# Output weights loaded early into a buffer of their own, and two extra products in the first step

## The chip, the cores and the metric

The kernel runs on one core of a Trainium2 chip. The metric is the time of one execution in microseconds of device time; the median of the runs shown counts. The profile is one execution more, with the hardware profiler on.

## The reference

Two attentions over the same rows of `x` (2048 x 448, 16 heads of 28), mixed by a gate. Branch A looks at 8 earlier positions, two apart; branch B is full attention.

```python
g = _sigmoid((x * gate_w).sum(-1, keepdims=True))
a = _A_ref(x, A_wqkv, A_wo)     # 8 positions, dilation 2, softmax, then @ A_wo
b = _B_ref(x, B_wqkv, B_wo)     # softmax(q k^T / sqrt(28)) v over all 2048, then @ B_wo
return g * a + (1 - g) * b
```

## The kernel before

**Stages.** Up to about 252 us TensorE (PE) makes the projections q, k, v of both branches. Then comes a loop of 256 steps, `st` = 0 to 255. Sixteen steps make a unit `u`: one group of four heads (`g = u // 4`) with one block of 512 queries (`b = u % 4`); a step takes 128 keys. Every number is split into a high and a low part, so that a product of two needs three matmuls. While units run, the output projection starts at step 237 and ends after the loop.

**One step.** PE makes the scores (12 products with `QH`, `QL`, `KH`, `KL`, line 1041) into the PSUM tiles `T`, and ahead of time up to three products (line 144) whose maximum VectorE (DVE) takes into `MX` (line 148), for the maxima of a later unit. ScalarE (ACT) makes `exp` of the scores (`P`, line 1044, two instructions in a step). Then `do_av` multiplies the probabilities of the step before with `V` into the tile `av` (line 995, 8 products). Step 0 has no step before it and so no `do_av`. From step 235 on the products ahead of time are done; from step 237 on `op_some` adds five parts of the output projection to a step (line 835, three products a part).

**Finishing a unit** (`fin_*`, with the list `l` of steps after the unit's end). For unit 13 the steps count from 224. `fin_copy` copies `av` to `osb`; `fin_sum` and `fin_sum2` write the sums of the softmax to DRAM (`rs<-osb`) and read them back spread out (`fsum<-rs`); `fin_inv` takes the reciprocal on DVE (`finv<-fsum`, line 864) and multiplies it by the gate on GpSimd (POOL, line 865); `fin_spread` and `fin_spread2` write it to DRAM (`rs<-finv`) and read it back broadcast (`rbc<-rs`); `fin_on` multiplies on POOL (`on<-osb,rbc`, line 903); `fin_hi` (`onhi<-on` on ACT, line 907) and `fin_lo` (`onlo` on POOL) split it, and `fin_store` writes it to `on_hi`, `on_lo`.

**Branch A** runs beside this on POOL and DVE, by a planner's lists. When its lists are empty, `a_done(st)` frees its buffers and plans the output weights: `wo` has 7 blocks of 128 rows. `raw_wo(k)` loads a block into one of 7 buffers of 512 columns, `split_wo(k)` splits it on POOL (lines 778 and 779). Branch A's turned rows, stored by eight transfers `oa_scr<-oatT`, are read back by `op_load_a(b)` into buffers of the same 7 (`oar`) and split by `op_split`. The rows of branch B come back by `op_load_b` (`onhi<-on_hi`, `onlo<-on_lo`).

**What sets the order.** Each engine executes its instructions in the order in which the program was written. `at(pos, st, f)` hangs a function on a place in step `st`: "pre", "dve", "act" or "end". All transfers of the loop are issued by SyncE's queue (SP), in program order, and one that must wait holds those behind it.

Of the kernel before, what the change touches and what calls it, by code (L numbers as in the profile page):

```python
# [8 lines left out]
F32 = mybir.dt.float32  # L9
# [6 lines left out]
S, D, H, DH = 2048, 448, 16, 28  # L16
# [4 lines left out]
NU = NG * NB  # L21
# [4 lines left out]
def gated_mix_kernel(ctx: ExitStack, tc: tile.TileContext, xT, xn, gw, wA, wB, woAB, out):  # L26
    nc = tc.nc
# [45 lines left out]
    KH = [cp.tile([128, S], F32R, name=f"KH{i}") for i in range(2)]  # L73
# [45 lines left out]
    def load_q(u):  # L119
        Qs[u] = load_part(u, "QH", qk_hi), load_part(u, "QL", qk_lo)  # L120
        for i in range(2):
            dma_r(Qs[u][0][DH + i::32, :], nm[u][16 * i:16 * i + 16, :].rearrange("(h q) c -> h (q c)", h=4))
# [61 lines left out]
    def max_turn(t):  # L184
        r = sp.tile([128, 32], F32, name="nms")
        nc.vector.transpose(r, t)
        return r

    def max_store(u, r):
        for a in range(4):  # L190
            nc.sync.dma_start(nm[u].bitcast(F32)[:, 32 * a:32 * a + 32], r[32 * a:32 * a + 32, :])
# [14 lines left out]
    with tc.tile_pool(name="xp", bufs=1) as xp, tc.tile_pool(name="wp", bufs=2) as wp:  # L206
# [244 lines left out]
        for n, t in enumerate(tiles):  # L451
# [4 lines left out]
            for w in splits:  # L456
                i, k = (n - splits[w][0]) * splits[w][1], splits[w][1]
# [36 lines left out]
            if parts and parts[0][0] <= n:  # L494
                _, u, t = parts.pop(0)
# [25 lines left out]
    def at(pos, st, f):  # L521
        hooks.setdefault((st, pos), []).append(f)

    def run(pos, st):
        for f in hooks.pop((st, pos), ()):
            f()
# [10 lines left out]
    av = pool.tile([128, 512], F32, name="av")  # L537
# [35 lines left out]
    maskt = mp.tile([128, W, NJ, 2], F32, name="maskt")  # L573
    ep = ctx.enter_context(tc.tile_pool(name="ep", bufs=1))
    probs = [ep.tile([128, 2, 512], F32, name=f"P{i}") for i in range(4)]
    nc.gpsimd.memset(maskt, 0.0)
    for st, g, t, src in ((12, 2, KH[2], qk_hi), (30, 1, KL[1], qk_lo), (72, 2, KL[0], qk_lo),
                          (100, 3, KH[0], qk_hi), (136, 3, KL[1], qk_lo)):
# [118 lines left out]
    for c in range(8):  # L697
# [20 lines left out]
        n = 0  # L718
# [37 lines left out]


    wo = []
    wor = {}
    oP = {}  # L760

    def rawtile(name):
        return oP["0"].tile([128, 512], F32, tag="raw", name=name)

    def load_wo():
        actx.close()
        oP["0"] = ctx.enter_context(tc.tile_pool(name="rp", bufs=7))
        oP["1"] = ctx.enter_context(tc.tile_pool(name="wop", bufs=1))
        oP["2"] = ctx.enter_context(tc.tile_pool(name="wop2", bufs=2))
        wo.extend(oP["1"].tile([128, 7, D], F32R, name=f"wo{i}") for i in range(2))  # L770

    def raw_wo(k):
        wor[k] = rawtile("wor")
        nc.sync.dma_start(wor[k][:, :D], woAB[k])

    def split_wo(k):
        raw = wor.pop(k)[:, :D]
        nc.gpsimd.tensor_copy(wo[0][:, k, :], raw)
        nc.gpsimd.tensor_tensor(out=wo[1][:, k, :], in0=raw, in1=wo[0][:, k, :].bitcast(F32), op=ALU.subtract)  # L779

    def a_done(st):
        adone.append(st)
        load_wo()

        for i, k in enumerate((4, 5, 6, 0, 1, 2, 3)):
            at("end", st + i // 2, lambda k=k: raw_wo(k))
            at("act", st + 3 + i, lambda k=k: split_wo(k))
        at("end", st + 6, lambda: op_load_a(0))

    oaT, onT = {}, {}  # L790

    def op_load_a(b):
        cs = slice(512 * b, 512 * b + 512)
        for k in range(4):
            n = 128 if k < 3 else 64
            raws[b, k] = rawtile("oar")[0:n, :]
            nc.sync.dma_start(raws[b, k], oa_scr[128 * k:128 * k + n, cs])

    def op_split(b, k):
# [13 lines left out]
    raws = {}  # L813
# [35 lines left out]
    def fin_copy(u):  # L849
        t = mp.tile([128, 512], F32, name="osb")  # L850
        nc.scalar.activation(t, av, AF.Copy)  # L851
        fin["o"] = t


    def fin_sum(u):
        nc.sync.dma_start(rs_scr[0][u].rearrange("(h c) -> h c", h=4), fin["o"][DH::32, :])

    def fin_sum2(u):
        fin["s"] = sp.tile([128, 16], F32, name="fsum")
        nc.sync.dma_start(fin["s"], rs_scr[0][u].rearrange("(p i) -> p i", i=16))  # L860
# [7 lines left out]
    def fin_spread(u):  # L868
        nc.sync.dma_start(rs_scr[1][u].rearrange("(p i) -> p i", i=16), fin["rec"])

    def fin_spread2(u):
        fin["r"] = mp.tile([128, 512], F32, name="rbc")
        for h in range(4):
            nc.sync.dma_start(fin["r"][32 * h:32 * h + 32, :],
                                rs_scr[1][u][512 * h:512 * h + 512].rearrange("(o c) -> o c", o=1).to_broadcast(
                                    [32, 512]))
# [28 lines left out]
    def fin_hi(u):  # L905
        fin["hi"] = mtile("onhi").bitcast(F32R)
        nc.scalar.activation(fin["hi"], fin["on"], AF.Copy)
# [5 lines left out]
    def fin_store(u):  # L913
        g, b = divmod(u, NB)
        for dst, t in ((on_hi, fin["hi"]), (on_lo, fin["lo"])):
            for h in range(4):
                r = 112 * g + DH * h
                dma_r(dst[r:r + DH, 512 * b:512 * b + 512], t[32 * h:32 * h + DH])

    def pool_time(t, f, *x):  # L920
        late["pool"] += t
        f(*x)


    for u in range(NU - 1):
        f = NJ * (u + 1)
        l = {NU - 3: (1, 2, 5, 6, 9, 12, 13, 15), NU - 2: (1, 2, 5, 6, 8, 10, 10, 12)}.get(
            u, (1, 3, 6, 8, 12, 18, 19, 22) if u < NU - 5 else (1, 3, 6, 8, 12, 15, 16, 19))
        at("pre", f + 1, lambda u=u: fin_copy(u))
        at("end", f + l[0], lambda u=u: fin_sum(u))  # L930
        at("end", f + l[1], lambda u=u: fin_sum2(u))
        at("dve", f + l[2], lambda u=u: pool_time(0.18, fin_inv, u))
        at("end", f + l[2], lambda u=u: fin_spread(u))
        at("end", f + l[3], lambda u=u: fin_spread2(u))
        at("end", f + l[4], lambda u=u: pool_time(1.24, fin_on, u, fin["r"]))
        at("pre", f + l[5], lambda u=u: fin_hi(u))
        at("end", f + l[6], lambda u=u: pool_time(1.24, fin_lo, u, nc.gpsimd))
        at("end", f + l[7], lambda u=u: fin_store(u))
# [6 lines left out]
    def s1_close():  # L945
        accs.extend(sums(1 - turn[0]))
        side["f"] = accs[1]
        order.extend([*pbank[0], *sums(turn[0])])
# [43 lines left out]
    def do_av(pv):  # L992
        kt, tiles_, g = pv
        for h in (3, 2, 1, 0):
            nc.tensor.matmul(av[32 * h:32 * h + 32, :], V[:, kt, 4 * g + h, :], tiles_[h],  # L995
                             start=(kt == 0), stop=(kt == NJ - 1), skip_group_check=True)
# [81 lines left out]
    for u in range(NU):  # L1078
        g, b = divmod(u, NB)
        for kt in range(NJ):  # L1080
            st = NJ * u + kt
            if kt == (8 if u < 12 else 12) and u + 1 < NU:
                load_q(u + 1)
            run("pre", st)
            issue("sp", st, 0)
            if st >= A_START:
                issue("pool", st, 4.2)
            if not adone and not any(lists.values()):
                a_done(st)
            cur = {}  # L1090
            left = s1e - s1c[0]
            for a in scores(u, kt, cur):
                if a == 2:
                    run("mid", st)
            run("dve", st)
            if u and kt == 6:
                late["dve"] += 0.25
            if finished:
                v = finished.pop(0)
                t = max_parts(v)  # L1100
                late["dve"] += 0.3
                late["pool"] += 0.18
                turned = {}
                lag = 2 if v < NU - 1 else 1
                at("dve", st + lag, lambda t=t, w=turned: w.update(r=max_turn(t.bitcast(F32))))
                at("end", st + lag, lambda v=v, w=turned: max_store(v, w["r"]))
            issue("dve", st, DLIM)
            issue("act", st, 0)
            run("act", st)
            if prev is not None:  # L1110
                do_av(prev)
            prev = (kt, cur, g)
            if OPS and st >= OPS[0]:
                op_some(st, 5)
            run("end", st)
            step = 2.25 if left else 2.1
            late["dve"] = max(0.0, late["dve"] + 0.58 * min(3, left) - step)
            late["pool"] = max(0.0, late["pool"] - step)
            if st == OP0 + 31:
                op_load_b(2, 3)  # L1120
            if not OPS and s1c[0] == s1e:
                s1_close()
                for k in range(4):
                    at("act", st + 1 + k // 2, lambda k=k: op_split(0, k))
                OPS.append(st + 3)
# [55 lines left out]
```

## Time and profile before

| | |
|---|---|
| median of 3 runs | 913.0 us (911.75, 913.0, 913.59) |
| the profiled execution | 914.46 us, of which its span 912.6 us |
| PE busy | 901.7 us, 99% of the span |
| DVE, ACT, POOL busy | 740.2, 645.9, 626.3 us |
| mean granted TensorE clock | 0.996 |

A row of a timeline has the start from the beginning of the span, how long it lasted, engine, line, operation, tiles, shapes and count; in brackets stands the idle time of the engine just before it and what ended it. Equal instructions in a row are merged: the second number is then the time from the first's start to the last's end. Matmuls overlap, so a merged row is more telling than the duration of one.

### The profile page before, as it was taken

Reading aid. Unit: us, or ns where it says so; the run is one execution under the profiler, and the core shown is the slowest. Engines: PE = TensorE matmul, PEld = TensorE weight load, DVE = VectorE, ACT = ScalarE, POOL = GpSimd, SP = SyncE. Lnnn points to the kernel's source line nnn. Section 1 sums busy time; section 2 is a strip of 40 time slices with the busy share of each in tenths; the row PEclk is TensorE's granted clock in tenths of the full one; section 3 lists DMA queues with packets and bytes.
Section 4 is the critical chain, followed back from the end, with each engine's and each line's share of the span. In section 5 each row is a group of like instructions: output and inputs, shape, how many; then the busy total and the mean of one; then the engine's idle time right before and its main releaser. Section 6 shows DMA issues by size and latency. Waiting matters only on the chain.

```text
span 912.6 us, 20606 instructions
## 1 busy us (share of the span) xinstructions
PE 901.7 (99%) x8332; PEld 534.0 (59%) x8332; DVE 740.2 (81%) x997; ACT 645.9 (71%) x775; POOL 626.3 (69%) x494
## 2 busy tenths in 40 slices
PE   9999999999999999999999999999999999899998
PEld 7899999999944444444444444444444444366667
DVE  6488999999979999999999999999999988610112
ACT  6456434343378898898888888888989888744550
POOL 2489846564479699998999998899999293600100
PEclk9999999999999999999999999999999999999999
DMA  9887403554373341244144322532222222664323
GB/s 273 288 258 197 133 11 90 156 131 115 82 243 71 102 113 48 88 106 122 32 120 133 104 82 47 137 95 56 80 53 46 55 55 43 201 187 130 98 89 102
DMA packets 113919, 104.30 MB, mean 114 GB/s; under 512 B 74708, under 2 KB 82260, under 8 KB 113040
## 3 DMA queue, kind: packets, MB, share of 16 engines
q1 hardware_dynamic: 113680, 102.72, 40.2%
q8 instruction: 65, 1.06, 0.5%
q10 hardware_dynamic: 144, 0.26, 0.1%
q14 instruction: 30, 0.25, 0.1%
HBM read 61.99 MB, written 40.48 MB: 112 GB/s over the span
## 4 chain that ended last, share of the span: by engine, by line
PE 91%; DMA 3%; SPq 2%; ACT 1%; issue 1%; DVE 1%; POOL 0%; ACTq 0%; DVEq 0%
PE T L1041 28%; PE av L995 26%; PE r L298 15%; PE r L293 7%; PE T L835 7%; PE r L144 5%; PE T L144 4%; DMA onlo<-on_lo 1%; ACT P L1044 1%; SPq L101 1%; DMA rs<-finv 1%; DMA V<-in_xT 1%; SPq L680 1%; DMA oar<-oa_scr 0%; POOL wo L779 0%
## 5 line engine op out<-in xcount | busy, mean ns | idle before, releaser
L1044 ACT ACTIVATE P<-T 128x1024 f32<-128x1024 f32 x512 | 497.2, 1025 | 100.5 <-PE T L1041 99.1
L148 DVE TENSOR_REDUCE MX<-T 128x1 f32<-128x512 f32 x470 | 440.2, 952 | 24.2 <-PE T L144 13.1
L995 PE MATMUL av<-P,V 128*32 128x512 f32 x2048 | 273.6, 606 | 1.1 <-ACT osb L851 0.7
L1041 PEld LDWEIGHTS T<-QH,KH 30*128 30x128 f32 x1024 | 91.1, 182 | 225.2 <-ACT P L1044 201.7
L144 PE MATMUL T<-KH,QP 28*128 28x512 f32 x704 | 219.8, 455 | 0.5 <-DVE MX L162 0.3
L1041 PE MATMUL T<-QH,KH 30*128 30x512 f32 x1024 | 212.3, 490 | 2.4 <-ACT P L1044 1.7
L162 DVE TENSOR_REDUCE MX<-r 128x2 f32<-128x1024 f32 x160 | 192.5, 1220 | 24.7 <-PE r L144 23.1
L1041 PE MATMUL T<-QH,KL 28*128 28x512 f32 x1024 | 186.6, 397 | 0.0
L1041 PE MATMUL T<-QL,KH 28*128 28x512 f32 x1024 | 184.2, 394 | 0.0
L614 POOL TENSOR_TENSOR prod<-qt,kt 128x896 f32<-128x896 f32 x64 | 135.3, 2116 | 0.4
L362 ACT ACTIVATE raw<-r 128x896 f32<-128x896 f32 (+1 forms) x64 | 58.9, 920 | 97.9 <-PE r L298 96.6
L668 POOL TENSOR_TENSOR oat<-oat,prod 128x896 f32<-128x896 f32 x56 | 118.1, 2109 | 2.7
L144 PEld LDWEIGHTS T<-KH,QP 28*128 28x128 f32 x704 | 86.1, 182 | 28.0 <-ACT P L1044 20.6
L663 POOL TENSOR_TENSOR prod<-vt,L 128x896 f32<-128x896 f32 x56 | 95.3, 1702 | 0.5
L363 POOL TENSOR_TENSOR ast<-raw 128x448 f32<-128x448 f32 x48 | 55.4, 1154 | 58.2 <-ACT raw L362 46.0
L1041 PEld LDWEIGHTS T<-QL,KH 28*128 28x128 f32 x1024 | 93.8, 185 | 0.0
L1041 PEld LDWEIGHTS T<-QH,KL 28*128 28x128 f32 x1024 | 92.3, 183 | 1.0
L995 PEld LDWEIGHTS av<-P,V 128*32 128x32 f32 x2048 | 40.3, 108 | 79.3 <-issue 72.7
L144 PE MATMUL r<-KH,QP 64*128 64x512 f32 x320 | 85.6, 390 | 0.0
L298 PE MATMUL r<-wh,xh 64*128 64x448 f32 (+1 forms) x512 | 84.8, 362 | 0.0
L298 PE MATMUL r<-wh,xl 64*128 64x448 f32 (+1 forms) x384 | 69.7, 363 | 0.0
L298 PE MATMUL r<-wl,xh 64*128 64x448 f32 (+1 forms) x448 | 65.7, 367 | 0.0
(114 smaller groups left out, 1038.6 us busy)
## 6 DMA issues: line engine op xcount, KB each, us to landing
a_scr<-ast SPq DMA_DIRECT2D x24, 448.0 KB
qk_hi<-qkh SPq DMA_DIRECT2D x24, 256.0 KB
qk_lo<-qkh SPq DMA_DIRECT2D x24, 256.0 KB
rbc<-rs SPq DMA_DIRECT2D x60, 64.0 KB
QP<-qk_hi SPq DMA_DIRECT2D x64, 56.0 KB
KL<-qk_lo SPq DMA_DIRECT2D x16, 224.0 KB
QH<-qk_hi SPq DMA_DIRECT2D x64, 56.0 KB
QL<-qk_lo SPq DMA_DIRECT2D x64, 56.0 KB
```

Source lines behind the costliest of these rows:

```text
L144: nc.tensor.matmul(bank, qhis[u][h % 2][r, 128 * qs:128 * qs + 128], KH[u // NB % 3][r, 512 * kc:512 * kc + 512], start=True, stop=True)
L148: r = nc.vector.tensor_reduce(MX[:, n % NMX:n % NMX + k], bank, axis=X, op=ALU.max)
L162: nc.vector.tensor_reduce(m, PM[k], axis=X, op=ALU.max)
L293: nc.tensor.matmul(bank, ws[c][rows, k, t[4]:t[4] + 128], x, start=first, stop=last)
L298: nc.tensor.matmul(bank[:, 0:cols], x, ws[c][rows, k, 0:cols], start=first, stop=last)
L614: nc.gpsimd.tensor_tensor(out=p, in0=qt[c], in1=kvt["k", c % 2][:, HALO - DIL * w:HALO - DIL * w + NJ, :], op=ALU.mult)
L663: nc.gpsimd.tensor_tensor(out=dst, in0=kvt["v", c % 2][:, HALO - DIL * w:HALO - DIL * w + NJ, :].rearrange("p j (h d) -> p j h d", d=DH), ...
L668: nc.gpsimd.tensor_tensor(out=oat[c], in0=oat[c], in1=oat[c, w], op=ALU.add)
L835: writes(bank, nc.tensor.matmul(bank[:, :D], src, wo[c][:, k, :], start=(first and k == ks[0] and i == 0), stop=(last and k == ks[-1] and ...
L995: nc.tensor.matmul(av[32 * h:32 * h + 32, :], V[:, kt, 4 * g + h, :], tiles_[h], start=(kt == 0), stop=(kt == NJ - 1), skip_group_check=True)
L1041: nc.tensor.matmul(bank[a], (KH[g % 3], KH[g % 3], KL[g % 2])[t][r, ks], (qh, ql, qh)[t][r, :], start=(t == 0), stop=(t == 2))
L1044: e = nc.scalar.activation(p, RP[0] if a == "2" else mine, AF.Exp, scale=SCALE).ins
```

## The change

- `rawt`, 7 blocks of 448 columns, is a buffer of its own. Two transfers load all raw output weights into it, blocks 4 to 6 at step 200 and blocks 0 to 3 at step 202, instead of seven transfers in the steps after `a_done`.
- The splits of the weights stand two to a step, beginning one step after `a_done` instead of three.
- Branch A's turned rows are read back into the first 2048 columns of `rawt`, and for the first block one step earlier.
- For unit 13, `fin_inv` and `fin_spread` stand one step later (6 instead of 5) and `fin_spread2` as well (7 instead of 6).
- In step 0, where there is no `do_av`, two products of 128x512 are written to `av`; the next `do_av` overwrites them.

```diff
+    rawt = ep.tile([128, 7 * D], F32, name="rawt")
...
-        oP["0"] = ctx.enter_context(tc.tile_pool(name="rp", bufs=7))
...
-    def raw_wo(k):
-        wor[k] = rawtile("wor")
-        nc.sync.dma_start(wor[k][:, :D], woAB[k])
+    def raw_wo(k0, k1):
+        nc.sync.dma_start(rawt[:, D * k0:D * k1].rearrange("p (k c) -> p k c", c=D),
+                          woAB[k0:k1].rearrange("k p c -> p k c"))
...
+    at("end", 200, lambda: raw_wo(4, 7))
+    at("end", 202, lambda: raw_wo(0, 4))
...
         for i, k in enumerate((4, 5, 6, 0, 1, 2, 3)):
-            at("end", st + i // 2, lambda k=k: raw_wo(k))
-            at("act", st + 3 + i, lambda k=k: split_wo(k))
-        at("end", st + 6, lambda: op_load_a(0))
+            at("act", st + 1 + i // 2, lambda k=k: split_wo(k))
+        at("end", st + 5, lambda: op_load_a(0))
...
-            raws[b, k] = rawtile("oar")[0:n, :]
+            raws[b, k] = rawt[0:n, 512 * k:512 * k + 512]
...
-        l = {NU - 3: (1, 2, 5, 6, 9, 12, 13, 15), NU - 2: (1, 2, 5, 6, 8, 10, 10, 12)}.get(
+        l = {NU - 3: (1, 2, 6, 7, 9, 12, 13, 15), NU - 2: (1, 2, 5, 6, 8, 10, 10, 12)}.get(
...
             if prev is not None:
                 do_av(prev)
+            else:
+                for _ in range(2):
+                    nc.tensor.matmul(av, KH[0][:, 0:128], KH[0][:, 0:512], start=True, stop=True, skip_group_check=True)
```

Three places show how instructions move. On SP's queue, from branch A's last stores to the first loads for the output projection, before (`wor` are the raw weights, `oar` the turned rows):

```order
L680 DMA oa_scr<-oatT 448x1x32 x8
L856 DMA rs_13_81<-osb 4x512
L774 DMA wor<-in_wo 128x448 x2
L860 DMA fsum<-rs_13_81 128x16
L774 DMA wor<-in_wo 128x448 x2
L101 DMA on_hi<-onhi 28x512 x4
L101 DMA on_lo<-onlo 28x512 x4
L774 DMA wor<-in_wo 128x448 x3
L869 DMA rs_13_97<-finv 128x16
L874 DMA rbc<-rs_13_97 32x512 x4
L101 DMA onhi_10229<-on_hi 64x512
```

The same stretch of SP's queue with the change:

```order
L681 DMA oa_scr<-oatT 448x1x32 x8
L854 DMA rs_13_81<-osb 4x512
L858 DMA fsum<-rs_13_81 128x16
L101 DMA on_hi<-onhi 28x512 x4
L101 DMA on_lo<-onlo 28x512 x4
L867 DMA rs_13_97<-finv 128x16
L795 DMA rawt<-oa_scr 128x512 x3
L795 DMA rawt<-oa_scr 64x512
L872 DMA rbc<-rs_13_97 32x512 x4
L101 DMA onhi_10227<-on_hi 64x512
```

The weights are gone from here, and the four loads of turned rows, which stood behind the first loads of `onhi` and `onlo`, now stand between `rs<-finv` and `rbc<-rs`.

On POOL, the first splits of the weights and the reciprocal's product of unit 13, before:

```order
L668 TENSOR_TENSOR oat_3316<-oat_3316,prod_9873 128x32x28
L911 TENSOR_TENSOR onlo<-on,onhi 128x512
L778 CAST wo_10024<-wor 128x448
L779 TENSOR_TENSOR wo_10025<-wor,wo_10024 128x448
L865 TENSOR_TENSOR finv<-finv,og 128x16
```

With the change all seven pairs of splits come first; this is the last pair and what follows it:

```order
L774 CAST wo_10026<-rawt 128x448
L775 TENSOR_TENSOR wo_10027<-rawt,wo_10026 128x448
L863 TENSOR_TENSOR finv<-finv,og 128x16
L901 TENSOR_TENSOR on<-osb,rbc 128x512
L181 TENSOR_TENSOR nmt<-nmv,nmt 128x16
L909 TENSOR_TENSOR onlo<-on,onhi 128x512
```

So `finv` moved from behind one split to behind seven.

On PE, the end of step 0 and the beginning of step 1 with the change:

```order
L144 MATMUL T_3275<-KH_152,QP_158 128x512
L144 MATMUL T_3275<-KH_152,QP_157 128x512
L1039 MATMUL T_3271<-QH,KL_153 128x512 x2
L1112 MATMUL av<-KH_151 128x512 x2
L1039 MATMUL T_3279<-QH,KH_151 128x512 x2
L144 MATMUL T_3283<-KH_152,QP_158 128x512
```

The row of line 1112 is new; nothing else moved on PE.

## Rows read from the trace of the kernel before

**Rows 1.** Timeline of PE, steps 1 to 3 of the loop

```profile
255.43 0.50 PE L1041 MATMUL T<-QH,KH 30*128 30x512 f32 x2 [0.66 <-ACT P L1044]
...
257.08 1.94 PE L995 MATMUL av<-P,V 128*32 128x512 f32 x8
...
260.54 1.06 PE L995 MATMUL av<-P,V 128*32 128x512 f32 x8
...
262.83 1.07 PE L995 MATMUL av<-P,V 128*32 128x512 f32 x8
```

**Rows 2.** Windows of 1 us, PE: busy (count), granted clock, DMA share, GB/s

```profile
255.00:256.00 1.00, 0.57 (x8) 1.00 0.02 5
...
257.00:258.00 1.00, 1.00 (x10) 0.50 1.07 242
```

**Rows 3.** Timeline of PE, four full-width products of the projection

```profile
10.45 1.09 PE L293 MATMUL r<-xh,wh 128*128 128x512 f32 x4
```

**Rows 4.** Timeline of PE, beginnings of steps 231 and 232

```profile
777.41 0.50 PE L1041 MATMUL T<-QH,KH 30*128 30x512 f32 x2
...
779.26 0.50 PE L1041 MATMUL T<-QH,KH 30*128 30x512 f32 x2 [0.63 <-DVE MX L148]
...
781.15 0.50 PE L1041 MATMUL T<-QH,KH 30*128 30x512 f32 x2
```

**Rows 5.** Timeline of DVE, the reciprocal of unit 13

```profile
777.28 0.25 DVE L864 RECIPROCAL finv<-fsum 128x16 f32<-128x16 f32 x1 [1.83 <-DMA fsum<-rs]
```

**Rows 6.** Chain that ended last: start, us, what ran or was waited for

```profile
770.72 2.25 DMA oa_scr<-oatT
...
780.53 5.40 DMA rs<-finv
...
793.68 5.99 DMA onlo<-on_lo
...
823.89 3.23 PE T L835 x15
```

**Rows 7.** Timeline of POOL, splits of the weights and unit 13

```profile
775.86 0.56 POOL L778 CAST wo<-wor 128x448 fp32r<-128x448 f32 x1 [14.08 <-DMA wor<-in_wo]
...
777.61 0.22 POOL L865 TENSOR_TENSOR finv<-finv,og 128x16 f32<-128x16 f32 x1
777.77 0.56 POOL L778 CAST wo<-wor 128x448 fp32r<-128x448 f32 x1
...
779.48 0.55 POOL L778 CAST wo<-wor 128x448 fp32r<-128x448 f32 x1
...
789.58 1.27 POOL L903 TENSOR_TENSOR on<-osb,rbc 128x512 f32<-128x512 f32 x1 [1.40 <-DMA rbc<-rs]
```

**Rows 8.** Timeline of ACT, steps 235 and 236

```profile
788.90 1.94 ACT L1044 ACTIVATE P<-T 128x1024 f32<-128x1024 f32 x2 [0.15 <-PE T L1041]
790.89 0.63 ACT L907 ACTIVATE onhi<-on 128x512 fp32r<-128x512 f32 x1
791.69 1.94 ACT L1044 ACTIVATE P<-T 128x1024 f32<-128x1024 f32 x2 [0.16 <-PE T L1041]
```

**Rows 9.** Timeline of PE, first products of the output projection, then step 238

```profile
796.19 0.65 PE L835 MATMUL T<-wo,onhi 128*128 128x448 f32 x2 [0.54 <-issue]
...
802.62 0.52 PE L1041 MATMUL T<-QH,KH 30*128 30x512 f32 x4
```

**Rows 10.** Timeline of SP's queue, unit 11

```profile
705.73 0.34 SPq L869 DMA_DIRECT2D rs<-finv  x1
707.22 1.69 SPq L874 DMA_DIRECT2D rbc<-rs  x4
```

**Rows 11.** Timeline of POOL, unit 11

```profile
715.31 1.28 POOL L903 TENSOR_TENSOR on<-osb,rbc 128x512 f32<-128x512 f32 x1
```

**Rows 12.** Windows, all engines: PE PEld DVE ACT POOL busy, clock, DMA, GB/s

```profile
793.00:794.00 1.00, 0.62 (x6) 0.30 (x8) 0.86 (x1) 0.62 (x1) 0.99 (x1) 1.00 0.93 297
...
800.00:801.00 1.00, 1.00 (x5) 0.87 (x3) 0.00 (x0) 0.00 (x0) 0.00 (x0) 0.50 0.29 100
```

More of the change, by code (lines that the diff above doesn't have):

```diff
@@ L758, in gated_mix_kernel @@
     wo = []
-    wor = {}
     oP = {}
-    def rawtile(name):
-        return oP["0"].tile([128, 512], F32, tag="raw", name=name)
     def load_wo():
         actx.close()
-        oP["0"] = ctx.enter_context(tc.tile_pool(name="rp", bufs=7))
         oP["1"] = ctx.enter_context(tc.tile_pool(name="wop", bufs=1))
@@ L770, in load_wo @@
         wo.extend(oP["1"].tile([128, 7, D], F32R, name=f"wo{i}") for i in range(2))
-    def raw_wo(k):
-        wor[k] = rawtile("wor")
-        nc.sync.dma_start(wor[k][:, :D], woAB[k])
+    def raw_wo(k0, k1):
+        nc.sync.dma_start(rawt[:, D * k0:D * k1].rearrange("p (k c) -> p k c", c=D),
+                          woAB[k0:k1].rearrange("k p c -> p k c"))
     def split_wo(k):
-        raw = wor.pop(k)[:, :D]
+        raw = rawt[:, D * k:D * k + D]
         nc.gpsimd.tensor_copy(wo[0][:, k, :], raw)
         nc.gpsimd.tensor_tensor(out=wo[1][:, k, :], in0=raw, in1=wo[0][:, k, :].bitcast(F32), op=ALU.subtract)
+    at("end", 200, lambda: raw_wo(4, 7))
+    at("end", 202, lambda: raw_wo(0, 4))
     def a_done(st):
```

## Prediction

> **What bounds the kernel now.** I read the page first: PE is busy for 99% of the span, so time can only be won where PE waits or where its clock is low. Then I looked for such places in PE's timeline, asked the windows for the clock, and followed each wait back over DVE, ACT, POOL and SP. Three places bear on this change.
>
> *Step 1.* PE waits 0.66 us for ACT [rows 1]. Within 2 us the granted clock is 0.50, that is 1.2 instead of 2.4 GHz [rows 2], and the eight `av` products that take 1.06 us elsewhere take 1.94 [rows 1].
>
> *Step 231.* PE waits for DVE's maxima [rows 4]. DVE itself stood 1.83 us at the reciprocal of unit 13, for `fsum<-rs` [rows 5].
>
> *Steps 236 to 238.* ACT's `onhi` of unit 13 stands between the exponentials of two steps, and its input arrives with no slack: `on` ends at 790.85 (789.58 + 1.27) [rows 7], and ACT is free at 790.84 (788.90 + 1.94) [rows 8]. Then the first 15 products of the output projection take from 796.19 to 802.62 [rows 9], while 15 undisturbed ones take 3.23 us; the chain shows that a load of `onlo` was awaited until 799.67 (793.68 + 5.99) [rows 6], and the clock is at 0.50 again [rows 12].
>
> **The two products in step 0.** Four products of this width take 1.09 us [rows 3], so two take at most 0.55 us. They stand before step 1's scores, in the wait of 0.66 us, and need nothing that PE has not waited for. They cost nothing; without that cover, 0.55 us.
>
> What they can give is the clock. From `av` of step 0 to `av` of step 1 it is 3.46 us (260.54 - 257.08), and the next distance is 2.29 [rows 1]: the low clock costs 1.17 us. With 0.55 us of the wait filled, 0.1 us stays idle. In step 231 a wait of 0.63 us did not bring the clock down: the 1.89 us from its end to step 232 (779.26 to 781.15) [rows 4] leave no room for products at half speed. So the place in step 1 is just beyond what brings the clock down, and I take it that the clock stays up: **-1.2 us**. The bounds are -1.2 and 0.
>
> The Trainium skill (TensorE: Matmul & The Clock Gate, section on HAM oscillation in real kernels) ties the low clock to long waits for transfers between bursts of products. By that page a wait as short as this would not bring the clock down, the fillers would have nothing to prevent, and this term would be 0. The trace shows the low clock right behind the short wait, so the row decides for the sum.
>
> **The early load.** Two transfers are issued at steps 200 and 202, of 0.69 and 0.92 MB. The first falls into the wait of SP between `rs<-finv` and `rbc<-rs` of unit 11 (705.73 to 707.22) [rows 10]. At 297 GB/s, as in a busy stretch [rows 12], both together take 5.4 us. The data of `rbc` are used at 715.31 [rows 11], 6.4 us after its last issue (707.22 + 1.69). So it costs 0; without that cover some 2 us on POOL, which waits for DVE there anyway.
>
> **The stall at step 231.** The weights no longer stand in front of `fsum<-rs`, and DVE's reciprocal stands a step later. The wait of 1.83 us was counted from a point one step (2.29 us) earlier than where it now stands, so it is gone even if the transfer is no faster. Step 231 took 3.74 us (781.15 - 777.41) [rows 4] instead of 2.29. That is **-1.45 us** for PE and ACT in steps 231 to 235.
>
> **Where that goes.** The splits of the weights may not begin before branch A's last store has landed, since `wo` takes the place of its buffers: 772.97 (770.72 + 2.25) [rows 6]. A split takes 1.71 us (779.48 - 777.77) [rows 7], seven take 12.0. So POOL reaches `finv` at 785.0, while before it did at 777.61, behind one split. `rs<-finv` is issued at 785.3 instead of 780.53 [rows 6]. It will land faster: before, it took 5.40 us with weights in the queues around it [rows 6], for unit 11 it let `rbc` go after 1.49 us [rows 10]. But four loads of turned rows are issued in between, at 0.42 us each by the rows of `rbc` (1.69 / 4): `rbc` is issued at about 787.35, and before at 785.93 (780.53 + 5.40). From that issue to `on` it was 3.65 us (789.58 - 785.93), so `on` starts at 791.0. The turned rows are 0.90 MB, 3.0 us at 297 GB/s, ahead of `rbc` in the same queue, which adds a little: **791.2**.
>
> `on` ends at 792.45, `onhi` at 793.1, and ACT begins the exponentials of step 236 at 793.15. Before it was 791.69 [rows 8]. ACT would be ready 1.45 us earlier than before, at 789.4, and so it stands for 3.1 us. The stall moves from DVE to ACT, and steps 236 and 237 come 1.46 us *later* than before.
>
> **The output projection.** Before, the 15 products began 4.50 us after those exponentials (796.19 - 791.69). After, that is 797.65, less the 0.54 us for which PE waited there [rows 9]: 797.1. Their operands are then there: the loads of `onhi` and `onlo` go out between 789 and 792, the last a good microsecond earlier than before. 15 products take 3.23 us. The clock will fall here as well, since PE now stands nearly 3 us in step 236. For its price I have 1.2 us from step 1 and, as the most, 2.4 us here (6.43 - 3.23, less 0.8 of waiting); I take 1.8. So step 238 begins at 802.1 instead of 802.62: **-0.5 us**, all told for steps 231 to 237. The bounds: at full clock 800.3 (-2.3); with a second fall 803.5 (+0.9). From step 238 to the end the order on PE is the same and PE is full, so what is won here stays.
>
> **The sum.** Against the profiled execution: 914.46 - 1.2 - 0.5 = 912.8. That execution lies 1.46 us above the median of 913.0, about one fall of the clock, and the three runs are spread over 1.8 us. Some of them may have had no fall in step 1, and in those the fillers win nothing. I count that term half against the median: 913.0 - 0.6 - 0.5 = **911.9 us**.
>
> **The rivals.**
>
> 1. *ACT does not wait.* This needs `on` done by 789.4, 3 us before my estimate, so the splits would have to begin earlier or take less. For it speaks that the weights lie ready long before; against it that `wo` takes the memory of branch A. Then steps 236 and 237 keep the 1.45 us, and the last operands, not ACT, set the projection: some 2.2 us before step 238. 913.0 - 0.6 - 2.2 = 910.2.
> 2. *The fillers do nothing*, because the clock falls for another reason than that wait. For it speaks that step 0 has few products with or without them. 913.0 - 0.5 = 912.5. The rule of the Trainium skill named above gives this time too; the trace has spoken against it once.
> 3. *Slower: `rbc` late.* If `rs<-finv` takes 5.40 us again, now because of 0.90 MB of turned rows behind it, `rbc` goes at 790.7, `on` starts at 794.3 instead of 791.2, and everything to step 238 is 3.1 us later: 913.0 - 0.6 - 0.5 + 3.1 = 915.0. Against it: the small transfer is issued ahead of them. `on` after 792.3 eats up all gains; after 794.1 the kernel is slower by more than 0.2%.
>
> That the stall of DVE stays is no rival in time: while ACT waits for `on`, 1.45 us on PE before it change nothing.
>
> **How the numbers follow.** My forecast has 0.55, rival 1 0.17, rival 2 0.20, rival 3 0.08. Two runs of this kernel can be told apart from about 0.2%, 1.8 us: faster means below 911.2, slower above 914.8. My forecast's own range is 910.8 to 913.0, by the price of the clock; a fifth of it counts as faster, with nearly all of rival 1 and a little of rival 2: 0.30. Slower is most of rival 3 with a second fall of the clock: 0.07. The rest, 0.63, is no change that can be told. The range of 909.9 to 914.0 takes in rivals 1 and 2 and the upper bound of the clock's price, and leaves out rival 3.
>
> **What the profile would show.** Right: no low clock in steps 1 and 2 and `av` at even distances; no wait of DVE for `fsum` in step 230; seven pairs of splits on POOL without a gap, then `finv`; ACT idle about 3 us ahead of line 907's successor, released by POOL's `on`, and PE idle with it; the first projection products without waits for loads. Wrong: splits that begin before branch A's stores have landed; `onhi` without idle time ahead of it; a clock of 0.50 still in step 1. What would make the number wrong is above all the clock in steps 236 to 238, whose price I know only to a microsecond either way.

## The result, and the profile after

The changed kernel takes **915.81 us** (median of 10 runs, 915.11 to 916.35); the kernel before took 912.9 us beside it (10 runs, 910.41 to 913.59). The ratio is 1.0035, 95% interval 1.0025 to 1.0044: slower by a third of a percent. The forecast was 911.9 us, with a range up to 914.0. The profiled execution took 915.27 us, its span 913.4 us.

The timeline of PE in the changed kernel, steps 1 to 3 and then the beginnings of steps 231 and 232:

```profile
254.56 0.73 PE L1112 MATMUL av<-KH 128*128 128x512 f32 x2
256.73 1.06 PE L993 MATMUL av<-P,V 128*32 128x512 f32 x8
258.93 1.06 PE L993 MATMUL av<-P,V 128*32 128x512 f32 x8
261.17 1.06 PE L993 MATMUL av<-P,V 128*32 128x512 f32 x8
...
776.25 0.50 PE L1039 MATMUL T<-QH,KH 30*128 30x512 f32 x2
...
778.40 0.50 PE L1039 MATMUL T<-QH,KH 30*128 30x512 f32 x2
```

Against [rows 1] the first `av` takes 1.06 us instead of 1.94 and the next follows after 2.20 us instead of 3.46. Against [rows 4] step 231 takes 2.15 us instead of 3.74. In DVE's timeline the reciprocal has no idle time in brackets any more, where it waited 1.83 us [rows 5]:

```profile
776.36 0.24 DVE L862 RECIPROCAL finv<-fsum 128x16 f32<-128x16 f32 x1
```

So both intended gains are there. They are lost five steps later. POOL's timeline, the first split, the reciprocal's product and `on` (compare [rows 7]):

```profile
772.09 0.56 POOL L774 CAST wo<-rawt 128x448 fp32r<-128x448 f32 x1 [11.50 <-DVE MX L148]
...
784.19 0.23 POOL L863 TENSOR_TENSOR finv<-finv,og 128x16 f32<-128x16 f32 x1
792.33 1.26 POOL L901 TENSOR_TENSOR on<-osb,rbc 128x512 f32<-128x512 f32 x1 [7.91 <-DMA rbc<-rs]
```

SP's queue between the two: the store of `finv`, the four turned rows, and only then `rbc`:

```profile
784.45 0.34 SPq L867 DMA_DIRECT2D rs<-finv  x1
784.83 1.93 SPq L795 DMA_DIRECT2D rawt<-oa_scr  x4
786.87 1.91 SPq L872 DMA_DIRECT2D rbc<-rs  x4
```

ACT stands behind `on` for 5.56 us, where it did not wait at all [rows 8]:

```profile
786.12 1.94 ACT L1042 ACTIVATE P<-T 128x1024 f32<-128x1024 f32 x2
793.62 0.63 ACT L905 ACTIVATE onhi<-on 128x512 fp32r<-128x512 f32 x1 [5.56 <-POOL on L901]
794.16 1.92 ACT L1042 ACTIVATE P<-T 128x1024 f32<-128x1024 f32 x2
```

and PE behind ACT for 5.14 us. The first projection products then wait for no load (compare [rows 9]), but step 238 begins at 803.52:

```profile
795.22 1.71 PE L1039 MATMUL T<-QH,KH 30*128 30x512 f32 x4 [5.14 <-ACT P L1042]
...
799.58 1.12 PE L833 MATMUL T<-wo,onhi 128*128 128x448 f32 x2
...
803.52 0.50 PE L1039 MATMUL T<-QH,KH 30*128 30x512 f32 x4
```

The chain that ended last goes through this place as well; before, the store of `finv` and the load of `onlo` stood there [rows 6]:

```profile
788.36 3.81 DMA rbc<-rs
792.33 1.27 POOL on L901
...
799.65 3.94 PE T L833 x15
```

The windows of 1 us (columns as in [rows 12]) show the DMA engines full in the last microsecond in which `rbc` is issued (786.87 to 788.78), PE idle at full clock, and then the low clock while PE works:

```profile
788.00:789.00 1.00, 0.89 (x10) 0.49 (x10) 0.00 (x0) 0.06 (x1) 0.00 (x0) 1.00 1.02 383
...
791.00:792.00 1.00, 0.00 (x0) 0.00 (x0) 0.00 (x0) 0.00 (x0) 0.00 (x0) 1.00 0.80 207
...
794.00:795.00 1.00, 0.00 (x0) 0.00 (x0) 0.97 (x3) 1.00 (x2) 0.67 (x1) 0.61 0.83 299
...
800.00:801.00 1.00, 1.00 (x4) 0.87 (x4) 0.00 (x0) 0.00 (x0) 0.00 (x0) 0.50 0.50 156
801.00:802.00 1.00, 1.00 (x7) 0.91 (x6) 0.00 (x0) 0.00 (x0) 0.00 (x0) 0.97 0.18 51
```

**One number for the place.** From the beginning of step 231 to that of step 238 it was 25.21 us before (802.62 - 777.41) [rows 4, 9] and is 27.27 us now (803.52 - 776.25). Up to its beginning the changed kernel is 1.16 us ahead (777.41 - 776.25); in it, it loses 2.06. Below I call it the stretch and give it for each kernel. In the profiles of before, of the changed kernel and of all variants below it is 81.3 us from `av` of step 237 to `av` of step 254, so nothing more is won or lost behind it.

### The profile page after: what moved, and what is told of

Its sections match the earlier page's. It is cut to its first block, busy times and chain, and to the rows that moved or that the text cites. A ratio compares the mean times of both kernels' runs of the same rounds, so it can differ in the third digit from the quotient of the medians.

```text
span 913.4 us, 20598 instructions
## 1 busy us (share of the span) xinstructions
PE 900.1 (99%) x8334; PEld 530.2 (58%) x8334; DVE 740.7 (81%) x997; ACT 645.9 (71%) x775; POOL 626.4 (69%) x494
## 3 DMA queue, kind: packets, MB, share of 16 engines
q8 instruction: 65, 1.06, 0.5%
## 4 chain that ended last, share of the span: by engine, by line
PE 94%; ACT 2%; POOL 2%; DMA 1%; SPq 1%; DVE 1%; issue 0%; ACTq 0%; POOLq 0%; DVEq 0%
PE T L1039 29%; PE av L993 27%; PE r L298 15%; PE T L833 8%; PE r L293 7%; PE r L144 4%; PE T L144 4%; ACT P L1042 1%; POOL wo L775 1%; DMA V<-in_xT 1%; DMA rbc<-rs 0%; POOL wo L774 0%; DVE MX L148 0%; SPq L795 0%; POOL oat L594 0%
## 5 line engine op out<-in xcount | busy, mean ns | idle before, releaser
L144 PE MATMUL r<-KH,QP 64*128 64x512 f32 x320 | 83.1, 390 | 0.0
```

Source lines behind the costliest of these rows:

```text
L144: nc.tensor.matmul(bank, qhis[u][h % 2][r, 128 * qs:128 * qs + 128], KH[u // NB % 3][r, 512 * kc:512 * kc + 512], start=True, stop=True)
```

## The experiments

My theory after this result: `on` is late because of the way that `finv` takes to it, and all of the loss follows from that. Two things make it late, the seven splits ahead of `finv` on POOL and the turned rows ahead of `rbc` in SP's queue. The rivals: the fillers cost something, or the low clock after the wait is the loss.

**The fillers alone** (the kernel before, and the two products).

```diff
             if prev is not None:
                 do_av(prev)
+            else:
+                for _ in range(2):
+                    nc.tensor.matmul(av, KH[0][:, 0:128], KH[0][:, 0:512], start=True, stop=True, skip_group_check=True)
```

> The kernel before with the two filler products of step 0 alone. If they hold TensorE's clock up: no stretch at 0.50 in steps 1 and 2, av of steps 0 and 1 2.2 to 2.3 us apart in place of 3.46, and about 0.5 to 1.2 us less than before (half or all of one fall of the clock): 911.7 to 912.4 us. If the fillers cost: 913.4 us or more. If they do nothing: the median of before, with the low clock still in the trace.

Measured: 912.88 us, ratio 0.9997 (0.9988 to 1.0007). In its profile the clock is at 1.00 in step 1 and at the projection too. There the first projection product waits 1.01 us for the turned rows, and the stretch is all the same 24.19 us (801.08 - 776.89), 1.02 less than in the profile of before, with the same code there. The low clock at the projection is the main difference: the last six of these products take 2.44 us before, at a granted clock of 0.50, and 1.37 with the fillers alone, at 1.00:

```profile
800.25 2.44 PE L835 MATMUL T<-wo,KH 128*128 128x448 f32 x6
```

```profile
799.77 1.37 PE L835 MATMUL T<-wo,KH 128*128 128x448 f32 x6
```

**The change without the fillers.** The diff is that of the change without its last three added lines.

> The changed kernel without the two filler products. If the loss lies in steps 235 to 238 and the fillers gain: 0.5 to 1.2 us more than the changed kernel, 916.3 to 917.0 us. If the fillers are to blame for the loss: back to about 913 us.

Measured: 916.5 us, ratio 1.0035 (1.0024 to 1.0046), the ratio of the whole change. In the profile PE's timeline has the low clock back in step 1:

```profile
257.55 1.94 PE L993 MATMUL av<-P,V 128*32 128x512 f32 x8
```

Five of its eight runs have a mean granted clock of 0.994, and three of ten of the changed kernel. So the fillers do neither good nor harm that the times show, and the loss isn't theirs.

**The turned rows behind `rbc`.**

```diff
-        at("end", st + 5, lambda: op_load_a(0))
+        at("end", st + 6, lambda: op_load_a(0))
```

> The changed kernel with the turned rows read back one step later, so that rbc goes out ahead of them. Theory rows (0.9 MB ahead of rbc in SP's queue makes rbc land late): rbc issued 0.9 us earlier and landing 3.7 us after its issue in place of 5.5, so ACT's wait at onhi of 5.56 us shrinks by about 2.7 us, and the time falls by 2 to 4 us to 912 to 914 us. Theory splits (finv behind seven splits on POOL is all of it): ACT still waits over 5 us, and the time stays at 915.8 us.

Measured: 914.38 us, ratio 1.0020 (1.0010 to 1.0031). `finv` begins on POOL as late as in the changed kernel (784.32), but `rbc` is issued 1.42 us after `rs<-finv` (785.99 - 784.57) instead of 2.42, and `on` begins 3.50 us after that instead of 5.46. SP's queue, POOL, and ACT behind it:

```profile
784.57 0.34 SPq L867 DMA_DIRECT2D rs<-finv  x1
785.99 1.69 SPq L872 DMA_DIRECT2D rbc<-rs  x4
```

```profile
789.49 1.27 POOL L901 TENSOR_TENSOR on<-osb,rbc 128x512 f32<-128x512 f32 x1 [4.94 <-DMA rbc<-rs]
```

```profile
790.79 0.63 ACT L905 ACTIVATE onhi<-on 128x512 fp32r<-128x512 f32 x1 [2.73 <-POOL on L901]
```

ACT's wait is halved. By the medians some two fifths of the loss are won back (1.0020 for 1.0035; the two intervals overlap). In the profiled execution, which lies 0.8 us above its median, nothing is: its stretch is 27.30 us, because `onhi` and `onlo`, loaded behind the rows, are now late for PE at the projection, and the clock falls twice there:

```profile
798.42 0.65 PE L833 MATMUL T<-wo,onhi 128*128 128x448 f32 x2 [0.84 <-DMA onhi<-on_hi]
```

**The splits later, the rows behind them.**

```diff
-            at("act", st + 1 + i // 2, lambda k=k: split_wo(k))
-        at("end", st + 5, lambda: op_load_a(0))
+            at("act", st + 4 + i // 2, lambda k=k: split_wo(k))
+        at("end", st + 7, lambda: op_load_a(0))
```

> The changed kernel with the splits of the weights three steps later in the program (two a step from step 229), so that finv on POOL stands behind two splits instead of seven, and the turned rows read back after the last split. Both theories: finv on POOL at about 776.6 instead of 784.2, rbc landed before the splits end, on at about 785.5, no wait of ACT at onhi, and steps 236 to 238 some 5 to 7 us earlier: 908.5 to 911 us. If a split that is late now holds the output projection instead (rows or weights not there when it begins), a wait of PE appears at its first products and it is 911 to 914 us. If theory rows alone were right this would be about as the run with the rows behind, 912 to 914 us, with ACT's wait of about 2.8 us still there.

Measured: **908.62 us**, ratio 0.9947 (0.9933 to 0.9960); in a second comparison 908.51 us, 0.9946 (0.9933 to 0.9958). It beats both kernels. `finv` now stands behind two splits and `on` behind the last one, with no wait:

```profile
777.50 0.22 POOL L863 TENSOR_TENSOR finv<-finv,og 128x16 f32<-128x16 f32 x1 [1.14 <-DVE finv L862]
...
786.32 1.29 POOL L901 TENSOR_TENSOR on<-osb,rbc 128x512 f32<-128x512 f32 x1
```

On SP's queue the rows are issued after `rbc`, and early enough:

```profile
780.91 1.70 SPq L872 DMA_DIRECT2D rbc<-rs  x4
...
785.00 2.21 SPq L795 DMA_DIRECT2D rawt<-oa_scr  x4
```

ACT passes `onhi` without a wait, and the clock stays at 1.00 at the projection. The stretch is 19.90 us (796.97 - 777.07), 5.3 less than before. ACT, then PE at its two ends:

```profile
786.94 1.94 ACT L1042 ACTIVATE P<-T 128x1024 f32<-128x1024 f32 x2
788.76 0.63 ACT L905 ACTIVATE onhi<-on 128x512 fp32r<-128x512 f32 x1
```

```profile
777.07 0.50 PE L1039 MATMUL T<-QH,KH 30*128 30x512 f32 x2
...
796.97 0.50 PE L1039 MATMUL T<-QH,KH 30*128 30x512 f32 x4
```

**`finv` on DVE** in the changed kernel: it no longer waits for the splits, while the rows stay ahead of `rbc`.

```diff
-            nc.gpsimd.tensor_tensor(out=r, in0=r, in1=og[:, u % NB, :], op=ALU.mult)
+            (nc.vector if u == NU - 3 else nc.gpsimd).tensor_tensor(out=r, in0=r, in1=og[:, u % NB, :], op=ALU.mult)
```

> The changed kernel with unit 13's product finv times gate done by VectorE, so that it waits for no split on POOL; the turned rows still stand between rs<-finv and rbc. Theory A (the turned rows block: their buffer is free only when the last split is done, 784.2, and SP holds rbc behind them): rs<-finv goes out at about 777, rbc all the same not before 786, on at about 791.7 instead of 792.3, ACT still waits about 5 us, 915 to 916 us. Theory B (finv behind the splits alone makes rbc late): rbc goes out at about 779, ACT's wait at onhi is gone, 909 to 911 us.

Measured: 912.76 us, ratio 1.0003 (0.9994 to 1.0012) and so neither of the two times expected. SP's queue and POOL (the second half of the fifth split, and `on`) show why:

```profile
777.49 0.34 SPq L867 DMA_DIRECT2D rs<-finv  x1
780.91 4.35 SPq L795 DMA_DIRECT2D rawt<-oa_scr  x4
785.35 1.92 SPq L872 DMA_DIRECT2D rbc<-rs  x4
```

```profile
779.74 1.15 POOL L775 TENSOR_TENSOR wo<-rawt,wo 128x448 fp32r<-128x448 f32 x1
...
790.34 1.26 POOL L901 TENSOR_TENSOR on<-osb,rbc 128x512 f32<-128x512 f32 x1 [5.99 <-DMA rbc<-rs]
```

`finv` is stored 7 us earlier, but the rows go into the columns of the raw weights, and the fifth split (of block 1) ends at 780.89 (779.74 + 1.15), where the first of them goes out. The four take 4.35 us instead of 1.93, and `rbc` waits behind them. From its issue to `on` it is 4.99 us. So the two causes aren't additive: the rows carry the splits' lateness to `rbc` even when `finv` is early.

**The wait filled with products.** In the changed kernel, 22 products of 128x512 into a tile `T` that is free then, at the end of step 236.

```diff
+            if st == 236:
+                for _ in range(22):
+                    nc.tensor.matmul(T1, KH[0][:, 0:128], KH[0][:, 0:512], start=True, stop=True)
             run("end", st)
```

> The changed kernel with 22 filler products of 128x512 into a free bank at the end of step 236, where TensorE waits 5.1 us for ACT. They leave the wait as it is and keep the clock up. If the low clock behind the wait costs what the rows of the changed kernel suggest (av 1.94 in place of 1.06, scores 0.5 more, the first 15 projection products 3.94 in place of 3.2): 1.7 to 2.2 us less, 913.6 to 914.2 us, and no stretch at 0.50 after step 236. If the low clock costs nothing beside the wait: 915.8 us.

Measured: 914.17 us, ratio 1.0014 (1.0006 to 1.0023). ACT still waits 5.53 us, but the clock stays at 1.00 through all of the loop; the mean of each of the 11 runs is 0.999 or 1.000, and of each of the ten runs of the changed kernel 0.994 or 0.996. From the exponentials of step 236 to step 238 it is now 7.10 us:

```profile
794.64 1.92 ACT L1042 ACTIVATE P<-T 128x1024 f32<-128x1024 f32 x2
```

```profile
801.74 0.51 PE L1039 MATMUL T<-QH,KH 30*128 30x512 f32 x4
```

In the changed kernel it is 9.36 (803.52 - 794.16). So the low clock there costs 2.26 us in the profiles, 1.6 between the medians (915.81 - 914.17), and without it the kernel is still slower than before. It is a part of the loss and comes from the wait.

**Two trims of the version with later splits.** Without the fillers:

> The kernel with the later splits (908.6 us) without the two filler products of step 0; its runs lie close together, so that it can tell the fillers' worth. In the traces with fillers av of step 20 came 0.4 to 0.8 us earlier after av of step 0 than in those without. So 0.4 to 0.8 us more, 909.0 to 909.4 us; if the whole fall of the clock counted, 1.2 us more, 909.8 us; if the fillers do nothing, 908.6 us.

Measured: 908.44 us, 0.9956 (0.9942 to 0.9969), no difference to the version with them, and the low clock of step 1 that I had expected did not come: the profile has full clock in step 1 although PE waits as in [rows 1]:

```profile
255.57 0.50 PE L1039 MATMUL T<-QH,KH 30*128 30x512 f32 x2 [0.66 <-ACT P L1042]
...
257.01 1.06 PE L993 MATMUL av<-P,V 128*32 128x512 f32 x8
```

And with POOL's memsets of branch A's buffers (`maskt`, `oat`) moved from the loop's beginning to the end of step 2. In the changed kernel, with PE at full clock, DVE stands 0.88 us in step 3 behind them:

```profile
261.09 0.21 DVE L186 STREAM_TRANSPOSE nms<-nmt 128x32 f32<-128x32 f32 x1 [0.88 <-POOL nmt L181]
```

> The kernel with the later splits, and POOL's clearing of maskt and of the two oat tiles (which waits 3.4 us for the projection's last stores) moved behind step 2, so that nmt of unit 1 on POOL does not stand behind it. If DVE's wait of 0.88 us for nmt in step 3 is where a part of the fillers' gain is given back: that wait is gone, av of step 4 comes 9.1 instead of 9.35 to 9.4 us after av of step 0 or better, and the time falls by 0.3 to 0.6 us to 908.0 to 908.3 us. If not, 908.6 us.

Measured: 907.99 us, 0.9948 (0.9935 to 0.9960). That wait is gone, and `av` of step 4 comes 8.91 us after `av` of step 0 instead of 9.37, but the time can't be told from 908.6.

**The reciprocal early again**, in the version with later splits. It asks what took DVE's stall away.

```diff
-        l = {NU - 3: (1, 2, 6, 7, 9, 12, 13, 15), NU - 2: (1, 2, 5, 6, 8, 10, 10, 12)}.get(
+        l = {NU - 3: (1, 2, 5, 7, 9, 12, 13, 15), NU - 2: (1, 2, 5, 6, 8, 10, 10, 12)}.get(
```

> The version with later splits, but with the reciprocal of unit 13 and its store back in the step in which they stood before (5 steps after the unit instead of 6). Nothing of the weights stands near the load of fsum now. Theory A, the weights in the queue made that load late: DVE waits for fsum 0.5 us at most, steps 230 and 231 stay even to half a microsecond, and the time is that of the version with later splits, 908.6 us, give or take 0.6. Theory B, it is the step later that took the stall away: DVE waits 1.5 to 1.9 us again, PE loses about 1.4 us in step 231, and since ACT no longer waits behind it in step 236, it shows in the time: 910.0 us.

The version with later splits beside it:

> The version with later splits once more, beside the one with the early reciprocal. Theory A: both within 0.6 us of each other, 908.6 us. Theory B: this one 1.4 us faster than the other.

Measured: 908.87 us (0.995, 0.9936 to 0.9964) beside 908.51. DVE does not wait, a step earlier than in the change:

```profile
775.23 0.24 DVE L862 RECIPROCAL finv<-fsum 128x16 f32<-128x16 f32 x1
```

So it was the weights in front of `fsum<-rs` that made the stall. With them gone the later step buys nothing.

## Why the prediction was wrong

The signs of the steps up to step 235 were right: the clock in step 1 (-1.26 us in the profile, -1.17 forecast; 0.76 of it is left at `av` of step 20, 45.42 us after that of step 0 instead of 46.18), the stall of DVE (step 231 shorter by 1.59, forecast 1.45), seven pairs of splits without a gap (12.10 us to `finv`, forecast 12.0), and a wait of ACT in step 236, with PE behind it. The two products took 0.73 us and not 0.55, but cost nothing, as forecast: step 1 begins 2.64 us after step 0 (255.29 - 252.65), before 2.63 (255.43 - 252.80). The reason that I gave for the low clock, a wait just beyond what brings it down, did not hold: waits of 0.66 us (later splits, no fillers) and of 1.01 us (the fillers alone) were followed by full clock.

Two terms of the sum were mis-sized, the first above all, and the step from the profile to the median failed.

**The way from `finv` to step 238 was mis-sized.** Counted from the beginning of step 231, in us:

| term | forecast | measured |
|---|---|---|
| first split (before step 231) | -4.44 | -4.16 |
| first split to `finv` | 12.03 | 12.10 |
| `finv` to the issue of `rbc` | 2.35 | 2.68 |
| issue of `rbc` to `on` | 3.85 | **5.46** |
| `on` to ACT's step 236 | 1.95 | 1.83 |
| from there to step 238 | 8.95 | 9.36 |
| step 231 to step 238 | 24.69 | 27.27 |

Counted from the forecast's own beginning of step 231, step 238 comes at 804.68 (777.41 + 27.27), past its bound of 803.5. Of the 2.6 us, 1.6 are one sentence: "which adds a little", 0.2 us for the turned rows ahead of `rbc`. By my own numbers 3.0 us of transfer, less the 1.7 us in which they are issued, leave 1.3 in front of `rbc`; I had them in hand and wrote 0.2. (The rows are 448 x 512 numbers, 0.92 MB and not 0.90, so it is 3.1 and 1.4.) Without the rows ahead it was 3.65 us from the issue to `on` [rows 6, 7] and 3.50 with the rows behind; with them it is 5.46 here and 4.99 with `finv` on DVE. While the last of `rbc` was issued the DMA engines were busy for all of the window that is shown above (1.02). The Trainium skill (DMA: Bandwidth & Descriptors, section on queues, rings and completion order) says that each DMA engine takes up the pieces of one queue in the order of the ring; the four durations are in line with it. In effect this is rival 3, `rbc` late, by another way than the one I gave for it: the store of `finv` did not slow down, the load that reads it back did.

**The clock** behind the wait was priced at 1.8 us; filling the wait shows 2.26. I had taken one fall. The low clock lasts from 794.2 to 801.1, as long as the two falls of before together, and covers all of step 237. That is 0.4 us of the table's last term. That it lasts so long because PE is idle for 5.1 us instead of 3 is not shown: with `finv` on DVE 6.8 us at 0.50 follow a wait of 2.67 us, with the rows behind `rbc` 3.4 us one of 2.31 us.

**The step from the profile to the median.** I forecast 912.8 for the profiled execution and took 0.9 off, because the profile of before lay 1.46 us above its median. By the table, the profile's account closes: 914.46 - 1.16 + 2.06 = 915.36, and 915.27 was measured. But the median of after lies above that. The terms -1.2 and -0.5 were measured against an execution of before with two falls of the clock, at a mean granted clock of 0.996. Of 54 more executions of the kernel before, measured beside the variants, 15 have 0.999 or 1.000, 19 have 0.998 and 20 have 0.996 or 0.997, with medians of 912.0, 912.7 and 913.5 us. So many have one fall and some none, while all ten of the changed kernel have 0.994 or 0.996. With the fillers alone, in an execution without any fall, the old code has a stretch of 24.19 us and takes 912.95. Against that the changed kernel is 0.64 us ahead at step 231 (776.89 - 776.25) and loses 3.08 in the stretch, 2.4 in all; the two profiled executions are 2.3 apart, the medians 2.9. So a part of what I counted as gain is something that many runs of before don't lose. How much of the error it makes is not shown.

What stays open: the kernels with the fillers and the early load reach step 231 between 776.24 and 777.25 in their profiles, and I don't know why. It doesn't enter the stretch.

## What to carry to other kernels

When a stall is removed, follow the next consumer that shares an engine or a queue with what was moved up: here work without a deadline (the splits) and a large load (the turned rows) were put ahead of a short chain with one (`finv`, `rs`, `rbc`, `on`), on POOL and on SP's queue at once, and each had to be moved for the gain to show (0.5% faster instead of 0.35% slower). A small load that is issued behind a large one in the same queue is counted behind what is left of the large one's time, not beside it (here 1.5 to 2 us more). And a gain measured against one profiled execution counts only if the stall in it is in the median as well.

## What the runs showed that I had not expected

- The fall of the clock in step 1 comes and goes with the same idle time: after a wait of 0.66 us the eight `av` products took 1.94 us in two profiles (before, and the change without fillers) and 1.06 in a third (the version with later splits, without them). The Trainium skill (TensorE: Matmul & The Clock Gate, Part 1) says that the number of slow products differs from run to run at a kernel's start; these three profiles show such a difference in the middle of one. None of the nine profiles with the fillers has a fall there.
- The five runs of the version with later splits lie within 1.0 us (907.88 to 908.83), 24 runs of before beside them within 4.2 (910.39 to 914.57). The five have a mean clock of 0.999 or 1.000, but the clock is not all of the spread: the nine of the 24 at 1.000 still lie between 910.39 and 912.9, and with the fillers alone the five at 1.000 (912.52 to 914.42) are no faster than the other six (910.96 to 913.37). What else moves the time is open.
